# A token-mixing MLP on one core: tile 1 becomes a column group, w1 is loaded in a half and two quarters, and the order is planned anew

## The chip, the cores and the metric

The kernel runs on one core of a Trainium2 chip. The metric is the device time in microseconds (us). Times of the kernel before come from 13 runs and from one profiled execution.

## What is computed

x is [2048, 512] in bf16, w1 and w2 [512, 512], w3 [512, 1792], w4 [1792, 512].

```python
h = gelu(layernorm(x) @ w1)
c = D // 4                      # four column blocks, shifted along the tokens by 1, -1, 2, -2
g0 = pad(h[:, :, 0:c],     token shift +1)
g1 = pad(h[:, :, c:2*c],   token shift -1)
g2 = pad(h[:, :, 2*c:3*c], token shift +2)
g3 = pad(h[:, :, 3*c:],    token shift -2)
x1 = x + concatenate([g0, g1, g2, g3]) @ w2
out = x1 + gelu(layernorm(x1) @ w3) @ w4
```

The pads are written in short form; the layernorm has no weights and an eps of 1e-5.

## The kernel before

The 2048 tokens are 16 tiles of 128. A tile of layer 1 is numbered 0 to 15; the same tile of layer 2, after the mixing, 16 to 31. All inputs and intermediate results stay in SBUF.

Steps of a tile in layer 1: load x; mean and variance (`ln`, L379), on VectorE (`bnst`, `bnag`) or with two accumulating passes on ScalarE (`sum`, `ssq`, then `msq` and `vpe` on VectorE); `rstd` on GpSimd (L416); the normalised tile (`norm`), on VectorE, ScalarE or GpSimd, the latter two with `nmr` = -mean x rstd ahead; its transpose into `xnT`, by TensorE (`pe_transpose`, L459, evicted by `ev`) or by a DMA transpose from SP (L455); `mm_up` (L569), the product with w1 in groups of 1, 2 or 4 tiles, with a gelu into `hT` on ScalarE. `mm_mix` (L610) multiplies four shifted windows of `hT` with w2 and adds x on VectorE, then the same `ln` for layer 2, `mm_up` with w3 into `h2T`, and `mm_down` (L642) with w4, whose sum with x1 goes out by DMA.

Tiles listed in `NAT` take another way: they are only centred (`norm` without rstd), transposed, and multiplied the other way round (`mm_up_rows`, L513: four matmuls of 512 columns), so that rstd can be the scale of the gelu (`gelur`, L538); the result is then transposed on TensorE (`h_transpose`, L544, step `th`) and copied into `hT` (`evh`). Tile 0, in `SPLIT`, does its first steps in two halves (`sa`, `sb`, `ra`, `rb`).

The order comes from three hands:

- TensorE runs `SCRIPT` word for word: `warm:n` is n matmuls on zeros, `ty`/`sa`/`sb` are transposes on TensorE, `ra`/`rb` the rows of tile 0, `up1:g` and `up2:g` the groups of `GROUPS`, `mix:t`, `down:t`.
- `LOADS` gives the order of loads on SP (or ACT, with `@act`), with some DMA transposes as fixed points between them; a load that stands behind `tpN` isn't issued before that transpose is. Loads come first on SP otherwise (`op.first`, L703).
- VectorE, ScalarE, GpSimd and the other SP work are placed by `Program.order` and `Program.place`: every operation gets a latest start, counted back from the TensorE script with its durations and hops (`HOP`), and the engine takes the earliest latest-start among what is ready within `LOOK`. The planner's figures for loads are `BEGIN`, `LAG` and `RESTART`. What comes out is a fixed order on each engine; at run time semaphores alone decide when each starts.

Tables say which engine does what for each tile: `NORM` (VectorE where nothing is said), `EVAC` for the eviction of transposes (ScalarE where nothing is said), `STAT_ACT`, `NMR`, `HEV`.

Of the kernel before, what the change touches and what calls it, by code (L numbers as in the profile page):

```python
# [6 lines left out]
P = 128  # L7
# [18 lines left out]
class Program:  # L26
# [2 lines left out]

    HOP = {"pe": 200.0, "dve": 155.0, "act": 220.0, "pool": 120.0, "sp": 70.0}  # L30
    LOOK = {"dve": 300.0, "act": 300.0}
    DUE = 252723.0
    BEGIN = {"sp": 30.0, "act": 150.0, "pe": 400.0, "dve": 150.0, "pool": 450.0}
    ENTRY = 1900.0
    COLD, RESTART = 4300.0, 800.0
    LAG = {"load": 150, "tp": 700}

    def __init__(self):
        self.ops = []
# [111 lines left out]
    def place(self, succs, order_only):  # L151
# [46 lines left out]
        def land(op):  # L198
            nonlocal moved, last
            if op.queue == "tp":  # L200
                at = max(clock + 500.0, op.start + 2450.0, last + 600.0) + self.LAG["tp"]
            elif op.name.startswith("out"):
                at = clock + 300.0
                self.total = max(self.total, at)
            else:
                moved += op.dur
                at = clock + 600.0 + min(600.0, 0.3 * moved) + (600.0 if op.dur > 1400.0 else 0.0) + self.LAG["load"]
            if op.queue != "tp":
                last = max(last, at)
            op.landed = at  # L210
            for j in succs[op.idx]:
                if (op.idx, j) not in order_only:
                    release(op, self.ops[j], at + 30.0)

        while len(out) < len(self.ops):
            while True:
                best = None
                for e in ENGINES:
                    if cands[e]:
                        t = max(free[e], min(ready[o.idx] for o in cands[e]))  # L220
                        if best is None or t < best[0]:
# [12 lines left out]
            if op.queue:  # L234
                tp = op.queue == "tp"
                free[e] = start + (1300.0 if tp else 500.0)
                load = op.name.startswith("dma")
                work = 600.0 if tp else op.dur + (self.RESTART if load and not fed.get(e, True) else 0.0)
                fed[e] = load
                rings[e].append([start + (1400.0 if tp else 1000.0), work, op])  # L240
                for j in succs[op.idx]:
                    if (op.idx, j) in order_only:
                        release(op, self.ops[j], None)
            else:
                dur = op.dur
# [21 lines left out]
BIAS = {}  # L267
LOADS = """
x0 w1a w1b x4-5 w2b tp2 x3 w2a x6-7 w3b x8 w3a x1@act x9 x2@act x11 tp16 w4a x10 tp11 w4b tp9 x12-14 x15
"""  # L270
SCRIPT = """
warm:8 sa:0 sb:0 ty:1 ra:0 rb:0 up1:1 ty:2 th:0-1 up1:2 mix:0 ty:4 ty:3 mix:1 up1:3 ty:5 up1:4 mix:2 up1:5
mix:3 ty:17 mix:4 up2:0 up1:6 up2:1 mix:6 down:1 mix:5 up1:7-8 mix:8 mix:7 up1:9 mix:10 down:0 down:2 mix:9
up1:10 mix:12 mix:11 up2:2 mix:13 down:3 down:6 mix:14 up2:3 mix:15 down:4-5 down:7 down:11 down:9-10 up2:4
down:8 down:12 down:14 down:13 down:15
"""

def bass_standalone__mixer_s_mlp__prompt_kernel(nc, x, w1, w2, w3, w4, out):
# [14 lines left out]
    with ExitStack() as es:  # L293
# [37 lines left out]
        def pair_rv(p, v):  # L331
            return [(("y", p, 0), v), (("y", p, 1), v)]
# [26 lines left out]
        def load(item):  # L359
# [153 lines left out]
        def mm_up_rows(t):  # L513
# [3 lines left out]
            def part(c0, c1):  # L517
# [5 lines left out]

                return f

            if t in SPLIT:
# [11 lines left out]
            pg.add("act", f"gelur{t}",  # L538
                   lambda e: e.activation(hn[:, k, :], y_ps[:, p, 0:D], ACT_F.Gelu_apprx_tanh,  # L539
                                          scale=rstd[:, t : t + 1]),  # L540
                   reads=pair_rv(p, v) + [(("rstd", t), 0), (("warm",), 1)], writes=[(("hn", t), 0)], dur=50 + D * 0.833)
            yield

        def h_transpose(t, pair):  # L544
            g = group_of[1, t]
            how = HEV.get(t, "act")
            k = NAT.index(t)
            if pair:
                b, v = next_pair()
                res, dst = pair_rv(b, v), y_bf[:, b, 0:D]  # L550
            else:
                b, v = next_bank()
                res, dst = [(("o", b), v)], o_bf[:, b, 0:D]

            def f(e):
                for c in range(DC):
                    ins = e.transpose(dst[:, P * c : P * (c + 1)], hn[:, k, P * c : P * (c + 1)], ident[:])  # L557
                return ins

            pg.add("pe", f"th{t}", f, reads=[(("hn", t), 0), (("ident",), 1)], writes=res, dur=225)  # L560
            to, frm = hT[:, :, 2 + P * t : 2 + P * (t + 1)], dst.rearrange("p (c s) -> p c s", s=P)
            pg.add(how, f"evh{t}",
                   (lambda e: e.activation(to, frm, ACT_F.Copy)) if how == "act" else
                   (lambda e: e.tensor_copy(to, frm)),
                   reads=res, writes=[(("h", j, g), 0) for j in range(DC)],
                   dur=(60 + 0.82 * D) if how == "act" else (75 + 0.51 * D))


        def mm_up(layer, g):  # L569
            t0, n = groups[layer][g]  # L570
# [123 lines left out]
        steps = [s for s in steps if s[0] not in ("th", "tz") or s[1] in NAT]  # L694
# [13 lines left out]
        for kind, n in steps:  # L708
            if kind == "warm":
                warm_pe(n)  # L710
            elif kind in ("sa", "ra"):
                halves[kind[0], n] = pe_transpose(n, n, True) if kind == "sa" else mm_up_rows(n)
                next(halves[kind[0], n])
            elif kind in ("sb", "rb"):
                next(halves[kind[0], n])
            elif kind in ("tp", "ty"):
                run(pe_transpose(n % NT, n, kind == "ty"))
            elif kind in ("th", "tz"):
                h_transpose(n, kind == "tz")
            elif kind == "mix":  # L720
                mm_mix(n)
            elif kind == "down":
# [107 lines left out]
```

## Time and profile before

| | |
|---|---|
| median of 13 runs | 135.44 us (134.97 to 136.0) |
| the profiled execution | 135.58 us; its span 134.2 us |
| TensorE busy | 130.7 us (97%), 780 matmuls |
| VectorE, ScalarE, GpSimd busy | 51.9, 58.5, 25.8 us |
| HBM | 6.82 MB read, 2.10 MB written |

The span runs from the first instruction to the last; the time of the execution has 1.4 us around it. In views of the profile PE is a matmul, PEld a weight load, DVE VectorE, ACT ScalarE, POOL GpSimd, SP SyncE; a q behind a name is the engine's own queue of instructions that aren't counted as busy, such as DMA issues. A line of a timeline or chain gives the start and duration in us, the engine, the line of the kernel, the operation, its output and inputs; the bracket is the idle time before it and what ended it. The end of a matmul is modelled.

### The profile page before, as it was taken

To read this page: it belongs to the slowest core of one execution; us is meant where nothing else is said; L and a number is where in the kernel's file an instruction comes from. 1 tells how busy PE (TensorE), PEld (TensorE's weight loads), DVE (VectorE), ACT (ScalarE), POOL (GpSimd) and SP (SyncE) were. 2 spreads that over 40 slices of the span, in tenths; PEclk is the share of its full clock that TensorE was granted. 3 is DMA by queue.
4 is the path that set the end of the run, shared out by engine and by line. 5 is a ranking of instruction groups with operands and counts; after the bars stand their busy time and mean duration, and the time that the engine had idled before them with its cause. 6 is when DMAs were issued, how large, how long until landed. Compare 5 with 4: busy or idle time off the path is not lost.

```text
span 134.2 us, 2013 instructions
## 1 busy us (share of the span) xinstructions
PE 130.7 (97%) x780; PEld 72.8 (54%) x792; DVE 51.9 (39%) x140; ACT 58.5 (44%) x90; POOL 25.8 (19%) x59
## 2 busy tenths in 40 slices
PE   8989999999999999999999999999999999999994
PEld 3468688885576446444444444444444444444463
DVE  2889999304947737700053400062222200012222
ACT  5698985669394303785520366600000155520000
POOL 2534467600865301300010310010000000000000
PEclk9999999999999999999999999999999999999999
DMA  6999398599056542111003110003112100001112
GB/s 186 365 389 350 56 316 142 100 288 244 11 107 82 118 82 75 39 39 39 5 0 78 39 39 0 0 0 85 39 39 73 45 0 0 0 5 39 39 39 78
DMA packets 21897, 12.32 MB, mean 92 GB/s; under 512 B 14464, under 2 KB 21376, under 8 KB 21888
## 3 DMA queue, kind: packets, MB, share of 16 engines
q1 hardware_dynamic: 21168, 11.80, 33.1%
q10 hardware_dynamic: 720, 0.39, 1.0%
q8 instruction: 6, 0.10, 0.3%
q14 instruction: 3, 0.02, 0.1%
HBM read 6.82 MB, written 2.10 MB: 66 GB/s over the span
## 4 chain that ended last, share of the span: by engine, by line
PE 97%; issue 1%; ACT 1%; DVE 0%; POOLq 0%; ACTq 0%
PE y_ps L586 45%; PE o_ps L655 36%; PE o_ps L626 10%; PE o_ps L679 3%; PE y_ps L520 2%; PE y_ps L482 1%; ACT hn L539 1%; PE o_ps L557 0%; DVE o_sb L663 0%; POOLq L815 0%; ACTq L779 0%
## 5 line engine op out<-in xcount | busy, mean ns | idle before, releaser
L586 PE MATMUL y_ps<-xnT,w_sb 128*128 128x256 bf16 (+2 forms) x421 | 62.4, 306 | 0.2
L586 PEld LDWEIGHTS y_ps<-xnT,w_sb 128*128 128x128 bf16 x424 | 39.0, 98 | 23.4 <-DVE xnT L490 0.3
L655 PE MATMUL o_ps<-w_sb,h2T 128*128 128x512 bf16 (+2 forms) x247 | 49.0, 355 | 0.3
L601 ACT ACTIVATE h2T<-y_ps 128x1024 bf16<-128x1024 f32 (+1 forms) x29 | 28.6, 993 | 42.6 <-PE y_ps L586 42.6
L655 PEld LDWEIGHTS o_ps<-w_sb,h2T 128*128 128x128 bf16 x252 | 23.6, 98 | 25.2
L663 DVE TENSOR_TENSOR o_sb<-o_ps,x_sb 128x512 bf16<-128x512 f32 (+2 forms) x18 | 11.4, 632 | 40.0 <-PE o_ps L655 39.9
L416 POOL TENSOR_TENSOR rstd<-mv,neghalf 128x1 f32<-128x1 f32 x21 | 11.6, 554 | 42.5 <-DVE mv L411 38.5
L626 PE MATMUL o_ps<-w_sb,hT 128*128 128x512 bf16 x60 | 15.2, 379 | 0.3
L409 DVE BATCH_NORM_STATS2 st<-x_sb 128x6 f32<-128x512 bf16 x21 | 14.2, 675 | 2.3 <-DMA x_sb<-in_x_dram 2.2
L637 DVE TENSOR_TENSOR x_sb<-o_ps,x_sb 128x512 bf16<-128x512 f32 x10 | 6.9, 687 | 12.7 <-PE o_ps L626 12.7
L633 DVE SCALAR_TENSOR_TENSOR x_sb<-o_ps,x_sb 128x512 bf16<-128x512 f32 x6 | 4.1, 690 | 16.8 <-PE o_ps L626 16.8
L601 ACT ACTIVATE hT<-y_ps 128x1024 bf16<-128x1024 f32 (+1 forms) x9 | 7.4, 827 | 6.3 <-PE y_ps L586 6.2
L416 POOL TENSOR_TENSOR rstd<-vpe,neghalf 128x1 f32<-128x1 f32 x11 | 6.0, 550 | 18.8 <-DVE vpe L405 18.7
L626 PEld LDWEIGHTS o_ps<-w_sb,hT 128*128 128x128 bf16 x64 | 6.0, 98 | 5.5
L437 DVE TENSOR_SCALAR xn_buf<-x_sb,mv,rstd 128x512 bf16<-128x512 bf16 x15 | 7.0, 468 | 4.8 <-POOL rstd L416 4.6
L446 ACT ACTIVATE xn_buf<-x_sb,nmr,rstd 128x512 bf16<-128x512 bf16 x8 | 6.5, 811 | 5.1 <-DVE nmr L442 3.2
L393 ACT ACTIVATE junk<-x_sb 128x512 bf16<-128x512 bf16 x11 | 6.8, 622 | 2.7 <-DVE x_sb L633 2.7
L449 POOL TENSOR_SCALAR xn_buf<-x_sb,rstd,nmr 128x512 bf16<-128x512 bf16 x7 | 5.3, 763 | 0.8 <-DVE nmr L442 0.4
L679 PE MATMUL o_ps<-zeros 128*128 128x512 bf16 x8 | 3.6, 631 | 0.6 <-POOLq L815 0.6
L411 DVE BATCH_NORM_AGGREGATE mv<-st 128x2 f32<-128x9 f32 x21 | 4.0, 191 | 0.2
L388 ACT ACTIVATE junk<-x_sb 128x512 bf16<-128x512 bf16 x5 | 3.1, 624 | 0.3 <-DMA x_sb<-in_x_dram 0.3
L482 PEld LDWEIGHTS y_ps<-ident,xn_buf 128*128 128x128 bf16 x28 | 2.3, 111 | 1.3 <-issue 0.6
(35 smaller groups left out, 30.8 us busy)
## 6 DMA issues: line engine op xcount, KB each, us to landing
w_sb<-in_w_dram SPq DMA_DIRECT2D x4, 896.0 KB, 6.5
out_dram<-o_sb SPq DMA_DIRECT2D x15, 128.0 KB, 1.7
w_sb<-in_w_dram SPq DMA_DIRECT2D x4, 256.0 KB, 4.6
x_sb<-in_x_dram SPq DMA_DIRECT2D x7, 128.0 KB, 5.1
x_sb<-in_x_dram SPq DMA_DIRECT2D x2, 256.0 KB, 4.9
xnT<-xn_buf SPq DMA_TRANSPOSE x25, 2.5
x_sb<-in_x_dram SPq DMA_DIRECT2D x1, 384.0 KB, 4.8
x_sb<-in_x_dram ACTq DMA_DIRECT2D x2, 128.0 KB, 3.3
```

Source lines behind the costliest of these rows:

```text
L393: (lambda d: (lambda e: e.activation(d, src, ACT_F.Square, accum_out=sums[:, q, 1:2])))(junk[:, b, :]),
L409: pg.add("dve", f"bnst{q}", lambda e: e.bn_stats(st9[:, q, 0:6], src), reads=rs, writes=[(("st", q), 0)], dur=605)
L416: lambda e: e.tensor_tensor(col(rstd), var, neghalf[:], ALU.pow),
L437: lambda e: e.tensor_scalar(dst, src, mv[:, q, 0:1], rstd[:, q : q + 1], ALU.subtract, ALU.mult),
L446: f = lambda e: e.activation(dst, src, ACT_F.Identity, bias=nmr[:, q : q + 1], scale=rstd[:, q : q + 1])
L586: ins = e.matmul(y_ps[:, p, W * i : W * (i + 1)], wsb[:, dc, P * fc : P * (fc + 1)], src[:, dc, P * t0 : P * t0 + W], start=(dc == 0), sto ...
L601: (lambda d, s: (lambda e: e.activation(d, s, ACT_F.Gelu_apprx_tanh)))(dst, ysrc),
L626: ins = e.matmul(dst, hT[:, j, c0 : c0 + P], w2_sb[:, j, :], start=(j == 0), stop=(j == DC - 1))
L637: f = lambda e: e.tensor_tensor(x1_sb[:, t, :], dst, x_sb[:, t, :], ALU.add)
L655: ins = e.matmul(dst, h2T[:, fc, P * t : P * (t + 1)], w4_sb[:, fc, cs], start=(fc == 0), stop=(fc == FC - 1))
L663: (lambda d, c: (lambda e: e.tensor_tensor(o_sb[:, oi, c], d, x1_sb[:, t, c], ALU.add)))(dst, cs),
L679: ins = e.matmul(o_ps[:, b, :], zeros[:, 0:P], zeros[:], start=True, stop=True)
```

## The change

- `NAT` shrinks from tiles 0 and 1 to tile 0. Tile 1 is now normalised in full (on ScalarE), and goes through `mm_up` as a group of one tile, 16 matmuls of 128 columns; `th:1` is gone. The copy of tile 0 into `hT` moves from ScalarE to VectorE (`HEV`).
- The first loads on SP are x1 and x2; x0 comes over ACT's queue. w1 comes as its first half, its fourth quarter and its third quarter; w2 as a half and two quarters, w3 and w4 as quarters. x7 to x10 come as one load. No load ahead of w4 stands behind a DMA transpose any more (tile 16 is transposed on TensorE); only tp7 stands in the list, ahead of x13 to x15.
- The warming matmuls go from 8 to 11. ty:2 now stands before the rows of tile 0.
- Groups of layer 1: six single tiles, then 2, 4, 2, 2. Groups of layer 2: 2, 4, 4, 4, 2 instead of 2, 2, 4, 4, 4, so that down:0 follows up2:0 and mix:4.
- The engine tables and the planner's figures change, and with them the order that the planner finds. `CSPLIT` is empty, so the code for it does nothing; `h_transpose` is a generator now and always uses a bank of `o_ps`, as `th:0` did.

```diff
-    DUE = 252723.0
-    BEGIN = {"sp": 30.0, "act": 150.0, "pe": 400.0, "dve": 150.0, "pool": 450.0}
+    DUE = 198048.0
+    BEGIN = {"sp": 30.0, "act": 560.0, "pe": 400.0, "dve": 150.0, "pool": 450.0}
-    LAG = {"load": 150, "tp": 700}
+    LAG = {"load": 750, "tp": 700}
...
-                at = clock + 600.0 + min(600.0, 0.3 * moved) + (600.0 if op.dur > 1400.0 else 0.0) + self.LAG["load"]
+                at = clock + 600.0 + min(600.0, 0.3 * moved) + (600.0 if op.dur > 1400.0 else 0.0)
+                at += self.LAG["load"] if moved > 1200.0 else 50.0
...
-                work = 600.0 if tp else op.dur + (self.RESTART if load and not fed.get(e, True) else 0.0)
+                dry = load and not fed.get(e, True) and clock + sum(h[1] for h in rings[e]) < start + 800.0
+                work = 600.0 if tp else op.dur + (self.RESTART if dry else 0.0)
...
-GROUPS = {1: (1, 1, 1, 1, 1, 1, 2, 2, 2, 2, 2), 2: (2, 2, 4, 4, 4)}
-NORM = {4: "act", 5: "act", 6: "act", 10: "act", 11: "pool", 12: "pool", 13: "act", 15: "act", 18: "pool", 20: "pool", 21: "pool", 22: "pool", 24: "act", 28: "act", 30: "pool"}
-EVAC = {1: "both", 2: "dve", 3: "dve", 7: "both", 9: "dve", 10: "both", 11: "both", 13: "both", 16: "dve", 17: "both", 19: "both", 20: "dve", 22: "both", 23: "dve", 24: "dve", 25: "dve", 28: "dve", 31: "dve"}
-STAT_ACT = (1, 6, 8, 9, 12, 21, 22, 23, 27, 28, 29)
+GROUPS = {1: (1, 1, 1, 1, 1, 1, 2, 4, 2, 2), 2: (2, 4, 4, 4, 2)}
+NORM = {1: "act", 5: "act", 6: "pool", 7: "pool", 8: "act", 9: "act", 10: "act", 11: "pool", 13: "pool", 18: "pool", 20: "pool", 21: "pool", 24: "act", 27: "pool", 28: "pool", 29: "pool"}
+EVAC = {0: "dve", 1: "both", 4: "both", 5: "both", 6: "dve", 7: "dve", 8: "both", 9: "both", 10: "dve", 11: "both", 15: "both", 17: "dve", 19: "both", 20: "dve", 21: "dve", 24: "both", 25: "both", 29: "dve", 30: "both", 31: "dve"}
+STAT_ACT = (0, 6, 7, 8, 9, 12, 13, 18, 21, 22, 25, 27)
...
-NMR = {0: "pool", 1: "pool", 3: "pool", 5: "pool", 7: "pool", 9: "pool", 10: "pool", 12: "pool", 13: "pool", 14: "pool", 17: "pool", 18: "pool", 19: "pool", 21: "pool", 22: "pool", 23: "pool", 27: "pool", 30: "pool"}
-NAT = (0, 1)
+NMR = {0: "pool", 2: "pool", 3: "pool", 4: "pool", 5: "pool", 6: "pool", 7: "pool", 8: "pool", 14: "pool", 16: "pool", 18: "pool", 22: "pool", 25: "pool", 26: "pool", 28: "pool", 31: "pool"}
+NAT = (0,)
 SPLIT = (0,)
-HEV = {2: "dve", 5: "dve", 6: "dve"}
-BIAS = {}
+CSPLIT = ()
+HEV = {0: "dve", 1: "dve", 2: "dve", 4: "dve", 6: "dve"}
+BIAS = {"msq0": -366.448}
 LOADS = """
-x0 w1a w1b x4-5 w2b tp2 x3 w2a x6-7 w3b x8 w3a x1@act x9 x2@act x11 tp16 w4a x10 tp11 w4b tp9 x12-14 x15
+x1 x2 w1a w1s w1r x3 x4 w2b x0@act w2q w2p x5 x6 tp5 w3r w3s x7-10 tp4 w3p tp5 w3q w4q w4p tp16 x12 w4r x11
+w4s tp7 x13-14 x15
 """
 SCRIPT = """
-warm:8 sa:0 sb:0 ty:1 ra:0 rb:0 up1:1 ty:2 th:0-1 up1:2 mix:0 ty:4 ty:3 mix:1 up1:3 ty:5 up1:4 mix:2 up1:5
-mix:3 ty:17 mix:4 up2:0 up1:6 up2:1 mix:6 down:1 mix:5 up1:7-8 mix:8 mix:7 up1:9 mix:10 down:0 down:2 mix:9
-up1:10 mix:12 mix:11 up2:2 mix:13 down:3 down:6 mix:14 up2:3 mix:15 down:4-5 down:7 down:11 down:9-10 up2:4
-down:8 down:12 down:14 down:13 down:15
+warm:11 sa:0 sb:0 ty:1-2 ra:0 rb:0 up1:1 th:0 up1:2 mix:0 ty:3 mix:1 ty:4 up1:3-4 ty:5 mix:2 ty:16 mix:3
+ty:17 up1:5 up2:0 mix:4 down:0 up1:6 down:1 up1:7 mix:5-6 up1:9 mix:10 mix:9 up1:8 mix:8 mix:7 up2:1 mix:11
+mix:13 up2:2 mix:12 down:5 down:2-3 mix:15 up2:3 mix:14 down:6 down:13 down:9 up2:4 down:4 down:10 down:7
+down:11 down:8 down:12 down:14-15
 """
...
-                c0, c1 = {"": (0, n), "a": (0, n // 2), "b": (n // 2, n)}[name[2:]]
+                cut = lambda k: k * n // 4
+                a, b = {"": (0, 4), "a": (0, 2), "b": (2, 4), "p": (0, 1), "q": (1, 2), "r": (2, 3), "s": (3, 4)}[name[2:]]
+                c0, c1 = cut(a), cut(b)
...
-        def h_transpose(t, pair):
+        def h_transpose(t):
```

A `tpN` in `LOADS` whose tile is transposed by TensorE is passed over (L698 to L700).

More of the change, by code (lines that the diff above doesn't have):

```diff
@@ L524, in part, with f @@
                 return f
+            if t in CSPLIT:
+                H = D // 2
+                for hh in (0, 1):
+                    cs = slice(H * hh, H * (hh + 1))
+                    def f(e, hh=hh, cs=cs):
+                        for dc in range(DC):
+                            ins = e.matmul(y_ps[:, p, 512 * hh : 512 * hh + H], xnT[:, dc, P * t : P * (t + 1)],
+                                           w1_sb[:, dc, cs], start=(dc == 0), stop=(dc == DC - 1))
+                        return ins
+                    pg.add("pe", f"rows{t}_{hh}", f,
+                           reads=[(("w1", c), 0) for c in range(DC)] + [(("xT", t, c), 1) for c in range(DC)],
+                           writes=[pair_rv(p, v)[hh]], dur=DC * 109.2)
+                    pg.add("act", f"gelur{t}_{hh}",
+                           (lambda a, b: (lambda e: e.activation(a, b, ACT_F.Gelu_apprx_tanh,
+                                                                 scale=rstd[:, t : t + 1])))(
+                               hn[:, k, cs], y_ps[:, p, 512 * hh : 512 * hh + H]),
+                           reads=[pair_rv(p, v)[hh], (("rstd", t), 0), (("warm",), 1)], writes=[(("hn", t, hh), 0)],
+                           dur=50 + H * 0.833)
+                    yield
+                return
             if t in SPLIT:
@@ L540, in mm_up_rows @@
                                           scale=rstd[:, t : t + 1]),
-                   reads=pair_rv(p, v) + [(("rstd", t), 0), (("warm",), 1)], writes=[(("hn", t), 0)], dur=50 + D * 0.833)
+                   reads=pair_rv(p, v) + [(("rstd", t), 0), (("warm",), 1)],
+                   writes=[(("hn", t, hh), 0) for hh in (0, 1)], dur=50 + D * 0.833)
             yield
-        def h_transpose(t, pair):
+        def h_transpose(t):
             g = group_of[1, t]
@@ L547, in h_transpose @@
             k = NAT.index(t)
-            if pair:
+            if t in CSPLIT:
                 b, v = next_pair()
-                res, dst = pair_rv(b, v), y_bf[:, b, 0:D]
+                steps = [(2 * hh, 2 * hh + 2, [pair_rv(b, v)[hh]], f"_{hh}") for hh in (0, 1)]
+                dst = y_bf[:, b, :].rearrange("p (k x) -> p k x", k=2)[:, :, 0 : D // 2]
+                chunk = lambda c: dst[:, c // 2, P * (c % 2) : P * (c % 2 + 1)]
+                part = lambda c0, c1: dst[:, c0 // 2, :].rearrange("p (c s) -> p c s", s=P)
@@ L551, in h_transpose @@
             else:
                 b, v = next_bank()
[L553 to L566, printed above, removed]
+                steps = [(0, DC, [(("o", b), v)], "")]
+                dst = o_bf[:, b, 0:D]
+                chunk = lambda c: dst[:, P * c : P * (c + 1)]
+                part = lambda c0, c1: dst.rearrange("p (c s) -> p c s", s=P)
@@ new lines, in h_transpose, with f @@
+            for c0, c1, res, tag in steps:
+                def f(e, c0=c0, c1=c1):
+                    for c in range(c0, c1):
+                        ins = e.transpose(chunk(c), hn[:, k, P * c : P * (c + 1)], ident[:])
+                    return ins
+                n = c1 - c0
+                pg.add("pe", f"th{t}{tag}", f,
+                       reads=[(("hn", t, hh), 0) for hh in range(c0 // 2, c1 // 2)] + [(("ident",), 1)],
+                       writes=res, dur=56 * n if n < DC else 225)
+                to, frm = hT[:, c0:c1, 2 + P * t : 2 + P * (t + 1)], part(c0, c1)
+                pg.add(how, f"evh{t}{tag}",
+                       (lambda a, b: (lambda e: e.activation(a, b, ACT_F.Copy)) if how == "act" else
+                        (lambda e: e.tensor_copy(a, b)))(to, frm),
+                       reads=res, writes=[(("h", j, g), 0) for j in range(c0, c1)],
+                       dur=(60 + 0.82 * n * P) if how == "act" else (75 + 0.51 * n * P))
+                yield
@@ L693, in bass_standalone__mixer_s_mlp__prompt_kernel @@
             steps += [(kind, n) for n in (range(int(a), int(b or a) + 1) if kind != "warm" else [int(n)])]
[L694 removed]
+        steps = [s for s in steps if s[0] != "th" or s[1] in NAT]
         pe_tp = {n for kind, n in steps if kind in ("tp", "ty", "sa")}
@@ L710, in bass_standalone__mixer_s_mlp__prompt_kernel @@
                 warm_pe(n)
-            elif kind in ("sa", "ra"):
-                halves[kind[0], n] = pe_transpose(n, n, True) if kind == "sa" else mm_up_rows(n)
+            elif kind in ("sa", "ra", "ta"):
+                halves[kind[0], n] = {"s": lambda n: pe_transpose(n, n, True), "r": mm_up_rows,
+                                      "t": h_transpose}[kind[0]](n)
                 next(halves[kind[0], n])
-            elif kind in ("sb", "rb"):
+            elif kind in ("sb", "rb", "tb"):
                 next(halves[kind[0], n])
@@ L717, in bass_standalone__mixer_s_mlp__prompt_kernel @@
                 run(pe_transpose(n % NT, n, kind == "ty"))
-            elif kind in ("th", "tz"):
-                h_transpose(n, kind == "tz")
+            elif kind == "th":
+                run(h_transpose(n))
             elif kind == "mix":
```

## The prediction

> **What bounds the kernel now.** I read the page's chain first (who ends last), then the chain in order of time (where it breaks), then the timeline of the first 9 us (why).
>
> ```profile
> PE 97%; issue 1%; ACT 1%; DVE 0%; POOLq 0%; ACTq 0%
> ```
>
> The end is set by TensorE alone; no other engine owns over 1% of the 134.2 us span. The chain in order of time shows where it isn't dense:
>
> ```profile
> 0.64 3.60 PE o_ps L679 x8
> 4.24 0.85 PE y_ps L482 x8
> 5.09 2.12 PE y_ps L520 x8
> ...
> 7.29 0.70 ACT hn L539
> ...
> 8.03 0.40 PE o_ps L557 x4
> 8.43 0.89 PE y_ps L586 x16
> 9.32 0.10 issue
> 9.42 0.81 PE o_ps L626 x3
> ...
> 17.26 13.97 PE y_ps L586 x128
> ```
>
> Prices per matmul follow: 128 columns 0.89/16 = 0.0556 us; 256 columns 13.97/128 = 0.109; 512 columns 0.2157 (14 of L655 in 3.02). From 9.32 (mix:0; an "issue" ahead of an "x3" is a matmul missing from the records) to 17.26 (up2:0) are 5 mixes (4.31), 4 tile transposes (0.90) and 3 single-tile ups (2.68): 7.89 of 7.94 us. From 17.26 to 132.41 the work priced so is 115.1 of 115.15 us. So **only the stretch before 9.32 holds idle PE time**: warming to 4.03, the wait of th1 for its gelu (7.2 to 8.03), and slow matmuls: 8 transposes take 0.85 instead of 0.45 us, 8 row matmuls 2.12 instead of 1.73.
>
> ```profile
> 2.61 0.69 DVE L409 BATCH_NORM_STATS2 st<-x_sb 128x6 f32<-128x512 bf16 x1 [2.02 <-DMA x_sb<-in_x_dram]
> 2.91 0.63 ACT L388 ACTIVATE junk<-x_sb 128x512 bf16<-128x512 bf16 x1 [0.31 <-DMA x_sb<-in_x_dram]
> 3.33 0.20 DVE L411 BATCH_NORM_AGGREGATE mv<-st 128x2 f32<-128x9 f32 x1
> 3.69 0.66 POOL L416 TENSOR_TENSOR rstd<-mv,neghalf 128x1 f32<-128x1 f32 x1 [1.99 <-DVE mv L411]
> 4.47 0.69 DVE L409 BATCH_NORM_STATS2 st<-x_sb 128x6 f32<-128x512 bf16 x1 [0.16 <-DMA x_sb<-in_x_dram]
> 5.44 0.11 PEld L520 LDWEIGHTS y_ps<-w_sb,xnT 128*128 128x128 bf16 x1 [0.31 <-DMA w_sb<-in_w_dram]
> 8.71 0.21 DVE L442 TENSOR_SCALAR nmr<-mv,rstd 128x1 f32<-128x1 f32 x1 [0.17 <-POOL rstd L416]
> 8.96 0.81 ACT L446 ACTIVATE xn_buf<-x_sb,nmr,rstd 128x512 bf16<-128x512 bf16 x1
> ```
>
> The last two lines are of a later tile, for the time that nmr and a ScalarE norm take. SP's first load (x0) is used at 2.61, ACT's first (x1) at 2.91, ACT's second (x2) at 4.47, w1's second half at 5.44.
>
> **What the Trainium skill says.** "TensorE: Matmul & The Clock Gate", Part 1: the array starts at half clock and is released by a free-running window of about 3.4 us, so the moment varies from run to run; cold 106.7/426.7 ns, warm 55.6/215.7 ns at 128/512 columns. The trace agrees: warming matmuls start 0.42 to 0.43 us apart, the transposes at 4.03 are 0.107 apart, and full pace comes only near 5.6. "Perfetto Trace Analysis", Tensor Engine Instruction: VectorE, ScalarE and GpSimd are strict FIFO; on this rests all I say of a wait holding what is queued behind it. "DMA: Bandwidth & Descriptors", Queues, rings and completion order: the DMA engines take turns between the SP and ACT rows. That fits x0 landing at 2.6 and x1 at 2.9.
>
> **The change, part by part.**
>
> *Start.* I follow the planner's rule (lowest latest-start first) by hand for the order on the engines, and take times from the trace only. x1 is now SP's first load: landed for use at 2.61. x0 is ACT's first: 2.91. x2 is SP's second: bounded by x1's 2.91 from below and by 4.47, what x2 took as ACT's second, from above. I take 3.6: the 393 KB of x0, x1, x2 are through about 2.7 by the page's GB/s, and landings trail by 0.7 to 1.2 us. VectorE: stats of x1 2.61 to 3.53, stats of x2 (0.69) to 4.29, then nmr1, which waits for rstd1 (3.69 + 0.66 = 4.35, + 0.10): 4.45 to 4.66; the mean of x2 to 4.75; norm0 in two halves to 5.15; norm2; ev0's halves. Queued behind the waiting nmr1 are that mean, norm0 and norm2, so sa:0, ty:2 and ra:0 wait for it.
> - ty:1: norm1 is now full and on ScalarE: 4.71 + 0.81 = 5.52, PE at 5.65. Before, centred-only on VectorE, done at 4.31.
> - ty:2: rstd2 4.9 to 5.45, norm2 (0.41) to 5.95, PE 6.1 to 6.3.
> - ra:0: ev0's first half runs after norm2, to 6.2; so rows at 6.3, before 5.02. Loss 1.3 us.
>
> *Warm 8 to 11.* Three more at 0.427 cold: 1.28 us, from 4.03 to 5.33 (0.65 if the clock has come). Norm0 allows sa:0 only at about 5.05, and ty:1 at 5.65; four half-transposes of 0.107 fit between, so the price is nothing. Cover gone: up to 1.28 us.
>
> *Tile 1 as a column group.* Four row matmuls (4 x 0.2157 = 0.86), gelur1 (0.69) and th1 (4 x 0.0556 = 0.22) go; 16 matmuls of 128 columns (0.89) come. Rows 6.3 to 7.16; up1:1 to 8.05 covers gelur0 (7.25 to 7.95, as gelur1 now follows its matmuls by 0.08); th0 to 8.27; up1:2 to 9.16. evh0, now on VectorE (0.42 instead of 0.60), is done by 8.9. So mix:0 starts at 9.16 to 9.3, before 9.32: **the removed gelu wait and cold pace (0.8 + 0.8) pay for the later start (1.3) and little more.** Gain 0.1.
>
> *tp16 to PE.* One tile transpose more after mix:0: + 0.22. Its DMA (SP issue 1.27) no longer stands ahead of w4.
>
> *Groups.* Two 256-column groups become one of 512 in layer 1: 32 x 0.1092 - 16 x 0.2157 = 0.04 gained. Up2 has the same 112 and 168 matmuls, reordered; downs, mixes and tail are the same count.
>
> *Loads.* w1 has the same seven 128 KB units ahead of its end, so it lands at about 5.43 as before; ra:0 and rb:0 need it at 6.3 and 6.7, so the split is worth 0 (cover gone: the excess over 6.7). One 128 KB unit costs (14.25 - 2.59)/32 = 0.364 us (33 units by x11's landing). w2 ends with unit 13, 7.0 to 7.9, needed at 9.2. w3 ends with unit 33, 14.3, needed at 16.4. w4 is no longer held behind tp16 and tp11; it ends with unit 49: 2.59 + 48 x 0.364 = 20.1. down:0 now comes right after up2:0 and mix:4 (16.4 + 6.1 + 0.9 = 23.4): cover 3.3 us. Moved past SP's queue: transposes follow all those loads; tp6 and tp7 are needed at 26.4, tp8 to tp11 at 31.2, at 1.3 us each. x13 to x15 wait behind tp7, needed only by up1:9 near 36. Cost 0 to 0.5; I take 0.
>
> *VectorE, 6.7 to 15.3.* ty:17 is due there at 15.3. Spaced as in the trace (stats 0.75, norm 0.33, x1 0.60, half eviction 0.20), stats of 3, 4, 5, 16, 17 (3.75), norms of 3, 4, 16, 17 (1.32), evh0 (0.34), three x1 (1.8) and two evictions (0.4) make 7.6 of 8.6 us; with waits for rstd I get ty:17 at 15.45. Cost 0 to 0.5, I take 0.15. Other stat, norm and rstd moves on ScalarE and POOL lie under 6 us of up2:0.
>
> *Sum* against the profiled execution (span 134.2, time 135.58): - 0.10 + 0.22 - 0.04 + 0.15 = **+0.2**, so 135.8. But that execution lies 0.14 over the median of 13 (135.44), and its slow clock lasted to 5.6 us, which costs the old order about half of the overlap with its work and the new one, which idles then, nothing. The early terms are good to 0.2 only; I write 135.5.
>
> **The rivals.** About 0.27 us (0.2%) is what a measurement of this kernel can tell from no change.
> - *Forecast: a tie*, 135.2 to 135.7. Chance 0.42.
> - *The start is quicker than my order.* If the mean of x2 goes ahead of nmr1, rstd2 starts at 4.35, norm2 ends at 5.45, rows start at 6.0 (ty:1 then limits) and no VectorE delay follows: 0.3 + 0.15 less, with tile 16's transpose in a gap of PE another 0.2: 135.5 - 0.5 = 135.0. For: POOL is free there. Against: nmr1 has the earlier due time. Chance 0.30.
> - *x2 lands late.* In VectorE's FIFO the stats of x2 stand before nmr1. From a landing of 3.76 on (4.45 - 0.69) each later us is lost once: at 4.47, as now, nmr1 is at 5.2, rows at about 7.0: + 0.7, 136.2; half as late 135.9. For: x2 took 3.8 us from issue in this trace. Against: it was second on ACT, now second on SP. With VectorE's delay at ty:17 it is the slower side. Chance 0.28.
> - *The w1 split is what it says but does nothing*: inside the tie.
>
> **How the numbers follow.** Chances are those of the three cases: faster 0.30, same 0.42, slower 0.28. The range reaches to 134.9 (quick start) and 136.2 (x2 as late as now); a w4 or transpose stall beyond is left out.
>
> **What would show it.** Rows (L520, four) starting near 6.3; mix:0 (first L626) near 9.2; up2:0 about 16.5; no DMA wait at the first L655 (down:0) near 23.4. Wrong if rows start below 5.9 or above 6.8, if PE waits for VectorE before ty:17 over 0.4 us, or if any wait breaks the chain after 17 us.

## The result, and where the time went

| | before | after |
|---|---|---|
| median | 135.41 us (134.95 to 136.14, 48 runs) | 137.02 us (136.22 to 138.37, 11 runs) |
| ratio | | 1.0119, 95% interval 1.0098 to 1.0141 |
| span, median of the runs | 134.1 to 134.4 us (by set of runs) | 135.4 us (134.5 to 136.5) |
| time around the span | 1.3 to 1.4 us | 1.3 us in 4 of 12 runs, 1.7 to 1.9 in 8 |
| profiled execution | 135.58 us, span 134.2 | 136.22 us, span 134.5 |

The change made the kernel slower by 1.6 us: 1.0 to 1.3 of span (by the set of runs of before that is taken), and 0.3 on average around it. Ratios and spans leave out the few executions in a slower state (here one of 12), while medians of the time keep them. The profiled execution of after happens to be the fastest of its runs, so it shows the loss in small; a repeat of the same kernel, below, shows it at its usual size.

The page's chain of after, shares of the span by engine:

```profile
PE 90%; ACT 4%; DVE 2%; DMA 2%; issue 1%; POOL 0%; DVEq 0%; SPq 0%
```

Before, TensorE had 97% here. The chain now leaves it in the first 17 us. The same chain in order of time, early and then around 16 us (start, duration, what):

```profile
0.09 2.36 DMA x_sb<-in_x_dram
4.41 0.82 ACT xn_buf L452
5.92 0.95 PE y_ps L526 x4
6.87 0.89 PE y_ps L624 x16
9.05 0.81 PE o_ps L664 x3
```

```profile
15.03 0.61 ACT junk L399 x2
15.63 0.62 ACT junk L394 x2
16.26 0.22 issue
16.48 6.27 PE y_ps L624 x56
```

The rows of tile 0 (L526, L520 before) start at 5.81 by the timeline, the first recorded matmul of mix:0 (L664) at 9.05, where before had it at 9.42, and up2:0 (the x56) at 16.48: close to the prediction's 6.3, 9.2 and 16.5. That up2:0 meets its forecast is luck, since a start 0.3 to 0.4 us quicker than forecast and a wait that wasn't forecast cancel. It could have started at 16.09, when the last matmul of up1:5 was issued and had run; TensorE stood for 0.39 us. The chain names ScalarE's statistics pass (L394) as what came before it. That pass is not an input of up2:0. The DMA view of the loads that SP issued between 7.82 and 7.90 us (only w3's last quarter; KB, then us from issue to landing) gives the real releaser:

```profile
w_sb<-in_w_dram SPq DMA_DIRECT2D x1, 448.0 KB, 8.3
```

Issued at 7.83, it landed at 16.13, where the prediction had w3 at 14.3. TensorE went on about 0.3 us later.

### The profile page after: what moved, and what is told of

Same layout as the page of the kernel before. It is cut to its first block, busy times and chain, and to the rows that moved or that the text cites. A ratio compares the mean times of both kernels' runs of the same rounds, so it can differ in the third digit from the quotient of the medians.

```text
span 134.5 us, 2020 instructions
## 1 busy us (share of the span) xinstructions
PE 131.0 (97%) x779; PEld 71.6 (53%) x791; DVE 52.0 (39%) x143; ACT 57.6 (43%) x92; POOL 27.6 (21%) x60
## 4 chain that ended last, share of the span: by engine, by line
PE 90%; ACT 4%; DVE 2%; DMA 2%; issue 1%; POOL 0%; DVEq 0%; SPq 0%
PE y_ps L624 43%; PE o_ps L693 36%; PE o_ps L664 9%; DMA x_sb<-in_x_dram 2%; ACT junk L399 1%; ACT junk L394 1%; PE y_ps L488 1%; PE y_ps L526 1%; ACT xn_buf L452 1%; ACT xnT L496 1%; DVE x_sb L671 1%; DVE st L415 1%; ACT hT L639 0%; POOL rstd L422 0%; DVE mv L417 0%
## 5 line engine op out<-in xcount | busy, mean ns | idle before, releaser
L624 PE MATMUL y_ps<-xnT,w_sb 128*128 128x512 bf16 (+2 forms) x420 | 63.6, 308 | 0.4 <-ACT junk L394 0.2
L624 PEld LDWEIGHTS y_ps<-xnT,w_sb 128*128 128x128 bf16 x424 | 38.3, 98 | 25.0 <-DVE vpe L411 0.4
L693 PE MATMUL o_ps<-w_sb,h2T 128*128 128x512 bf16 (+2 forms) x248 | 48.9, 355 | 0.2
L693 PEld LDWEIGHTS o_ps<-w_sb,h2T 128*128 128x128 bf16 x252 | 23.5, 98 | 24.9 <-issue 0.4
L675 DVE TENSOR_TENSOR x_sb<-o_ps,x_sb 128x512 bf16<-128x512 f32 x11 | 7.5, 684 | 22.0 <-PE o_ps L664 22.0
L664 PE MATMUL o_ps<-w_sb,hT 128*128 128x512 bf16 x60 | 14.9, 379 | 0.2
L415 DVE BATCH_NORM_STATS2 st<-x_sb 128x6 f32<-128x512 bf16 x20 | 13.6, 685 | 2.7 <-DMA x_sb<-in_x_dram 2.5
L639 ACT ACTIVATE hT<-y_ps 128x512 bf16<-128x512 f32 (+1 forms) x10 | 8.1, 810 | 6.6 <-PE y_ps L624 6.5
L664 PEld LDWEIGHTS o_ps<-w_sb,hT 128*128 128x128 bf16 x64 | 6.1, 98 | 6.0
L399 ACT ACTIVATE junk<-x_sb 128x512 bf16<-128x512 bf16 x12 | 7.5, 623 | 2.7 <-DVE x_sb L671 2.6
L455 POOL TENSOR_SCALAR xn_buf<-x_sb,rstd,nmr 128x512 bf16<-128x512 bf16 x10 | 7.6, 766 | 1.0 <-DVE nmr L448 0.4
L452 ACT ACTIVATE xn_buf<-x_sb,nmr,rstd 128x512 bf16<-128x512 bf16 x6 | 4.8, 811 | 0.9 <-DVE mv L417 0.9
L717 PE MATMUL o_ps<-zeros 128*128 128x512 bf16 x11 | 4.2, 558 | 0.6 <-POOLq L854 0.6
L394 ACT ACTIVATE junk<-x_sb 128x512 bf16<-128x512 bf16 x7 | 4.4, 623 | 0.7 <-DMA x_sb<-in_x_dram 0.7
L488 PE MATMUL y_ps<-ident,xn_buf 128*128 128x128 bf16 x32 | 3.0, 220 | 0.2 <-ACT xn_buf L452 0.2
```

Source lines behind the costliest of these rows:

```text
L399: (lambda d: (lambda e: e.activation(d, src, ACT_F.Square, accum_out=sums[:, q, 1:2])))(junk[:, b, :]),
L415: pg.add("dve", f"bnst{q}", lambda e: e.bn_stats(st9[:, q, 0:6], src), reads=rs, writes=[(("st", q), 0)], dur=605)
L452: f = lambda e: e.activation(dst, src, ACT_F.Identity, bias=nmr[:, q : q + 1], scale=rstd[:, q : q + 1])
L455: f = lambda e: e.tensor_scalar(dst, src, rstd[:, q : q + 1], nmr[:, q : q + 1], ALU.mult, ALU.add)
L624: ins = e.matmul(y_ps[:, p, W * i : W * (i + 1)], wsb[:, dc, P * fc : P * (fc + 1)], src[:, dc, P * t0 : P * t0 + W], start=(dc == 0), sto ...
L639: (lambda d, s: (lambda e: e.activation(d, s, ACT_F.Gelu_apprx_tanh)))(dst, ysrc),
```

## Where the loads fell behind

SP's timeline, before and then after: SP issues a load every 0.47 us or so, for 128 KB as for 896 KB.

```profile
0.09 0.40 SPq L365 DMA_DIRECT2D x_sb<-in_x_dram  x1
0.56 0.93 SPq L372 DMA_DIRECT2D w_sb<-in_w_dram  x2
1.53 0.47 SPq L365 DMA_DIRECT2D x_sb<-in_x_dram  x1
...
4.05 0.47 SPq L372 DMA_DIRECT2D w_sb<-in_w_dram  x1
```

```profile
0.09 0.87 SPq L369 DMA_DIRECT2D x_sb<-in_x_dram  x2
1.00 1.45 SPq L378 DMA_DIRECT2D w_sb<-in_w_dram  x3
2.49 0.91 SPq L369 DMA_DIRECT2D x_sb<-in_x_dram  x2
3.44 1.42 SPq L378 DMA_DIRECT2D w_sb<-in_w_dram  x3
4.89 0.91 SPq L369 DMA_DIRECT2D x_sb<-in_x_dram  x2
5.85 0.91 SPq L378 DMA_DIRECT2D w_sb<-in_w_dram  x2
```

The first part of w3 is issued at 4.05 us before and at 5.85 after. By 2.45 us the two queues of before had been given 1408 KB (x0 to x2, w1, x4-5, w2b), those of after 768 KB (x0 to x2, w1). The windows view shows what the DMA engines made of it; of each line read the last two figures, the DMA share and GB/s, before and then after:

```profile
2.00:3.00 1.00, 1.00 (x4) 0.35 (x3) 0.39 (x1) 0.68 (x3) 0.00 (x0) 1.00 1.06 346
3.00:4.00 1.00, 1.00 (x3) 0.18 (x2) 0.93 (x5) 1.00 (x3) 0.31 (x1) 1.00 1.03 356
4.00:5.00 1.00, 1.00 (x9) 0.84 (x9) 0.84 (x3) 0.76 (x4) 0.35 (x1) 1.00 1.07 375
```

```profile
2.00:3.00 1.00, 1.00 (x4) 0.34 (x3) 0.53 (x1) 0.33 (x2) 0.00 (x0) 1.00 0.81 241
3.00:4.00 1.00, 1.00 (x3) 0.30 (x2) 0.93 (x3) 0.52 (x2) 0.52 (x1) 1.00 0.68 174
4.00:5.00 1.00, 1.00 (x8) 0.46 (x6) 0.67 (x4) 0.59 (x1) 0.57 (x2) 1.00 1.00 325
```

In these three microseconds 1077 KB came before and 740 KB after: 0.34 MB, at before's 350 GB/s about 1 us of loading, is missing from then on. "DMA: Bandwidth & Descriptors", Issuing engines are not separate DMA queues, of the Trainium skill says that the time a sequencer needs to initiate a DMA is "usually small relative to the DMA itself". For 128 KB this case says otherwise: 0.47 us of issue against 0.36 us of data. That the issues are what kept the engines short here is not shown by this: a kernel with fewer of them, below, loads no faster in this stretch.

## The experiments

The theories, by the letters that some of the expectations use. D: the many small early loads make w3 and w4 late, and TensorE waits for them. N: over 64 loads and stores lengthen the time around the span. V and E: VectorE or ScalarE is late for up2:0, as the profile's lines say. C: the cold clock at the start. Each ratio is to the kernel before, with its 95% interval; the span is the median of the runs. The experiments add lines, so L624, L664 and L693 are L625, L666 and L695 in some.

**The kernel after again.** No edit.

> The changed kernel once more, unaltered, for a second profile, since the first profiled execution (span 134.5 us) was the shortest of twelve, whose spans reach 136.7. Median about 137.0 again. Theory W (the last quarter of w4 lands too late for down:0): a longer execution shows PE waiting for a DMA of w4 ahead of the first matmul of L693, 0.5 to 2 us. Theory C (the array's clock is released later than before, because the new start leaves TensorE idle or only transposing between 4.8 and 5.8): the first L717, L488 and L526 matmuls are at half pace until 7 us or later, and nothing waits at L693. Theory E (ScalarE and VectorE late ahead of up2:0): PE waits near 13 to 16.5 us for ScalarE, by more than the 0.4 us of the first profile.

137.19 us, 1.0115 (1.0073 to 1.0157), span 135.4, which is 1.0 over the kernel before in the same set of runs. The timeline of this run again blames another engine:

```profile
17.11 0.56 PEld L624 LDWEIGHTS y_ps<-xnT,w_sb 128*128 128x128 bf16 x6 [0.67 <-DVE x_sb L675]
17.14 0.71 PE L624 MATMUL y_ps<-xnT,w_sb 128*128 128x256 bf16 x5 [0.52 <-DVE x_sb L675]
```

The sum of L675 belongs to another tile than the two of up2:0. w3's last quarter, issued at 7.80, landed 9.0 us later, at 16.8; TensorE had been free since 16.45 (0.68 us, the bracket leaves out a matmul missing from the records).

**Waits taken away by other data.** The first kernel lets down:0 use w4's chunks 3 to 6 in place of 10 to 13; the second lets up2:0 use w3's chunk 0 in place of chunk 1; the third does both. The work of every engine and its order stay the same; what is left out is the wait for the loads of the chunks replaced. Of the edits only the operands are shown; the lists of what these matmuls wait for are shortened to match.

```diff
-    w4_sb[:, fc, cs]
+    w4_sb[:, fc - 7 if t == 0 and fc > 9 else fc, cs]
```
```diff
+    wc = 0 if layer == 2 and g == 0 and dc == 1 else dc
-    wsb[:, dc, P * fc : P * (fc + 1)]
+    wsb[:, wc, P * fc : P * (fc + 1)]
```

> The changed kernel, but down:0 multiplies its last four chunks with four other chunks of w4 (3 to 6), so that it doesn't wait for w4's last quarter; every load and the order of all engines stay. Tile 0's output is another one for this. Theory W: the excess goes, 135.4 to 135.8 us. Theories C and E: 137.0 us, within 0.3 of the changed kernel.

> The changed kernel, but up2:0 multiplies with chunk 0 of w3 in place of chunk 1, so that it doesn't wait for the quarter that lands last; every load and the order of all engines stay. Tiles 0 and 1 of the output are others for this. Theory D: PE's gap ahead of up2:0 shrinks to under 0.1 us, the median falls by 0.3 to 0.7, to about 136.5 us, if w4 doesn't take the time back at down:0. Theory V: no change, 137.0 us.

> The changed kernel with both waits for weights taken away: up2:0 as in the run with chunk 0 for chunk 1 of w3, and down:0 with chunks 3 to 6 of w4 for 10 to 13. Tiles 0 and 1 of the output are others for this. Theory D with w4 as a second late landing: median 135.6 to 136.1 us, the span's median within 0.3 us of the kernel before; what then is left over is the time around the span (1.3 or 1.8 us in the runs of the changed kernel, 1.3 in all of before). Theory V: 136.7 us, as with down:0 alone.

| free of | median | ratio | span | over before in the same set |
|---|---|---|---|---|
| w4's last quarter at down:0 | 136.72 us | 1.0069 (1.0044 to 1.0095) | 135.0 | 0.6 |
| w3's last quarter at up2:0 | 136.6 us | 1.0066 (1.003 to 1.0101) | 134.85 | 0.75 |
| both | 136.07 us | 1.0032 (1.0008 to 1.0055) | 134.45 | 0.35 |

With w4's wait alone gone, up2:0 still stood for 0.43 us in the profiled execution; w3 landed at 16.05 there.

TensorE's timeline with w3's wait gone: at 15.89 up1:5 now runs straight into up2:0, but down:0 (L695) starts 0.50 us after the end of mix:4 (the first of mix:4's four matmuls is missing; the bracket again names a bystander). w4's last quarter landed at 24.1 there.

```profile
15.89 1.93 PE L625 MATMUL y_ps<-xnT,w_sb 128*128 128x128 bf16 x24
...
23.11 0.81 PE L666 MATMUL o_ps<-w_sb,hT 128*128 128x512 bf16 x3
24.25 1.02 PE L695 MATMUL o_ps<-w_sb,h2T 128*128 128x512 bf16 x4 [0.33 <-DVE xn_buf L443]
```

With both gone it is dense:

```profile
15.31 7.17 PE L625 MATMUL y_ps<-xnT,w_sb 128*128 128x128 bf16 x72
22.53 0.81 PE L666 MATMUL o_ps<-w_sb,hT 128*128 128x512 bf16 x3
23.25 2.10 PE L695 MATMUL o_ps<-w_sb,h2T 128*128 128x512 bf16 x9
```

V and E fall: VectorE and ScalarE do the same work in the same order in all four kernels, and the stall at up2:0 goes with w3's semaphore alone. C falls as the cause of the loss: by the spacing of the matmuls full pace came near 5.6 us in the profiled execution of before and near 5.8 in the repeat of after, and the kernel with four pairs joined, next, starts as this repeat does (first recorded matmul of mix:0 at 9.40 and 9.42) without the loss. The moment does move from run to run: where w3's wait is gone full pace came only near 6.5, and mix:0 at 9.75. The two waits are worth 0.65 us of span together by the sets' own runs of before (1.0 to 0.35), 0.95 by the medians as they stand (135.4 to 134.45).

**Early pairs joined.** w1's two quarters, x3 and x4, w2's two quarters, x5 and x6 become one load each (64 loads and stores instead of 68). Every engine keeps its order.

`join` (its code is left out) gives the first load of a pair the range of both and drops the second, after the order has been planned.

```diff
+        for a, b in [('w1s', 'w1r'), ('x3', 'x4'), ('w2q', 'w2p'), ('x5', 'x6')]:
+            join(a, b)
```

> The changed kernel with the order of every engine kept, but four pairs of neighbouring loads on SP joined into one DMA each: w1's third and fourth quarter, x3 and x4, w2's two quarters, x5 and x6. Theory D (SP issues one load per 0.48 us whatever its size, so that ten loads of 128 KB ahead of w3 keep the DMA engines short of work, w3's last quarter lands at 16.1 to 16.8 us, and up2:0 waits for it): w3 is issued some 1.9 us earlier and lands 0.8 to 1.2 us earlier, PE's gap ahead of up2:0 (0.4 to 0.7 us) goes, and the median falls by 0.5 to 1.0, to 136.0 to 136.5 us. Theory V (VectorE and ScalarE are late ahead of up2:0, as the chain names them): the gap and 137.0 us stay.

135.81 us, 1.0027 (1.0011 to 1.0044), span 134.5, 0.4 over before in the same set: in the profiled execution TensorE doesn't wait ahead of up2:0 or down:0. The loads of w3 and w4 joined into halves instead, with the early ones left small, do much less:

> The changed kernel with the four pairs of quarters of w3 and w4 joined, and the small loads ahead of w3 left as they are (64 DMAs; w4's last quarter goes ahead of x11 by this). The order of all engines stays. Theory D: w3 is issued as late as in the changed kernel, so it lands no earlier than 16 us and PE waits ahead of up2:0 as there, span 135.0 to 135.4; with theory N 1.3 us around it, 136.4 us in all. Rival (the number of loads alone counts): as with the four early pairs joined, 135.8 us.

136.46 us, 1.0091 (1.0054 to 1.0128), span 135.15, 0.95 over before. w3 landed at 16.70 in the profiled execution, as theory D says, and up2:0 waited 0.26 us.

**Which pair?** Only w1's quarters joined, and only the other three pairs.

> The kernel after with only the two quarters of w1 joined (67 loads and stores instead of 68), every engine's order as it is. If the loss is in proportion to the issues that SP spends on small loads ahead of w3, one of the four that the joined kernel saved is saved here: span about 135.1 to 135.2 instead of 135.4, time about 136.7 to 136.9. If the split of w1 is itself the cause (its last quarter starves the rows and what follows), the span falls to the 134.5 of the kernel with four joins, and the time to about 135.9. If w1 is nothing to it, 137.1 as the kernel after.

> The kernel after with x3 and x4, the two quarters of w2, and x5 and x6 joined, w1 left in its half and two quarters (65 loads and stores). In proportion to the issues: span about 134.7, time 136.0 to 136.2. If w1's split is the cause: span 135.4, time 136.8 or more. The two runs together say whether the split that the change is named for is the costly one.

135.92 us, 1.0034 (1.0015 to 1.0053), span 134.55, and 135.95 us, 1.0043 (1.0025 to 1.0062), span 134.6. Taken alone, the first is what "w1's split is the cause" had foretold, and the second comes close to a sum over issues; together neither holds. It is no sum, since one join gives as much as three or four, and w1's split is not *the* cause, since the kernel that keeps it is as fast. It looks like a threshold. (The traced execution of the kernel with only w1 joined is one of its longest, 135.1 us of 133.9 to 135.2: up2:0 still waits 0.61 us there.)

**What the joins change.** D, as I had it, is at most half of the story. The trace keeps, for each load, when each of its 16 parts was complete. The table has, for the profiled execution of each kernel, the GB/s of 0 to 6 us and of 8 to 12 us (windows view), and for the last load of w3 its place among the loads of SP, when most of it was there (the 14th of the 16 parts) and when all of it was (us):

```
kernel                      0-6  8-12  place  most   last   last - most
before                      267  401   11th   12.95  13.69  0.74
before, early splits        232  336   15th   14.63  15.61  0.98
after                       209  346   17th   15.62  16.13  0.51
after again                 192  359   17th   15.40  16.79  1.38
free of w4 at down:0        202  353   17th   15.19  16.05  0.87
free of w3 at up2:0         212  300   17th   16.21  17.11  0.90
free of both                214  313   17th   15.86  18.07  2.21
w3 and w4 joined            196  314   15th   16.41  16.70  0.29
only w1 joined              196  375   16th   14.93  16.68  1.75
w2, x3-4, x5-6 joined       213  366   14th   15.53  15.81  0.28
four pairs joined           207  390   13th   15.19  15.40  0.21
four pairs, 9 warming       201  392   13th   14.95  15.01  0.05
four pairs, 8 warming       211  398   13th   14.97  15.26  0.30
```

The first 6 us are not what the joins mend. The kernels with the new order load 192 to 214 GB/s there with the pairs joined and without, against 267 before; over 6 us that is 0.3 to 0.45 MB, or about 1 us of loading at 350 GB/s. The windows of the kernel with four pairs joined, to be set beside those of after above:

```profile
2.00:3.00 1.00, 1.00 (x4) 0.33 (x3) 0.42 (x1) 0.24 (x2) 0.00 (x0) 1.00 0.76 231
3.00:4.00 1.00, 1.00 (x3) 0.30 (x2) 0.97 (x3) 0.61 (x2) 0.42 (x1) 1.00 0.78 201
4.00:5.00 1.00, 1.00 (x4) 0.43 (x3) 0.74 (x5) 0.49 (x1) 0.57 (x2) 1.00 1.02 331
```

By 2.45 us this kernel had been given 1152 KB, where after had 768, and it moved no more. So the early shortage is not shown to come from small loads. A rival is the order of the first loads: x2 now stands behind x1 on SP instead of on ACT's queue, and w1 behind both. No run changed that alone, so the cause of the early shortage stays open.

What goes with the joins comes later. From 8 to 12 us four joined pairs load at 390 to 398 GB/s and fewer joins at 366 and 375, against 300 to 359 without early joins. And the last parts come sooner. One or two of the sixteen parts lag behind the others by up to 2.2 us. The lag is not one load's: it rises at one, and then stays at about the same size for those that follow (1.61 to 1.78 us over ten loads where only w1 is joined) until it is gone at w4's last quarter. Without early joins (but for w3 and w4 joined), and with only w1 joined, it rises between SP's 12th and 14th load, ahead of w3's end; with three or four pairs joined it rises at the 15th (w4: 0.22 to 0.93 us with four pairs), behind w3's end. TensorE was ready for w3 at 16.0 to 16.7 us where it had to wait, so most of the parts came in time or nearly so, and in most of these kernels the lag decides. The early shortage explains why the cover is thin, the late parts why it is then exceeded. The kernel before has late parts too, 0.7 us in its profiled execution; w3 lands there at 13.7, over 3 us ahead of its use.

The same loads can give different lags: 0.51, 1.38 and 0.87 us in the three kernels that load exactly as after does up to w3's end and wait for it, and 0.7 us in before but 0.2 in the kernel below that differs from it only in late loads. So chance has a share, and with one traced execution for each kernel the place where the lag rises is an observation, not a law. Why it rises when it does wasn't isolated. "DMA: Bandwidth & Descriptors", Latency and other measured facts, of the Trainium skill says that two of the sixteen DMA engines, 7 and 15, are usually slower than the others; its guess at the cause is limited to DMAs issued by GpSimd, which these loads are not. One or two late parts fit that, but the records don't say which engine did which part.

**The same splits in the kernel before.** w1b, x4-5, w2a and x6-7 become two loads each (67 loads and stores instead of 63), orders kept.

> The kernel before with four of its early loads cut in two: w1's and w2's second in line into quarters, x4-5 and x6-7 into single tiles (67 DMAs), the order of all engines kept. Theory D (small loads keep the DMA engines short of work): the DMA engines have moved some 0.15 to 0.3 MB less by 7 us, w3's last half lands 0.5 to 1 us later than 13.7, but up2:0 needs it only at 17.1, so the span stays within 0.3 us. With theory N 1.8 us around the span in half of the runs. Rival (w3's late landing comes from the order of the loads, not from their size): landing at 13.7 as before.

136.95 us, 1.0084 (1.0053 to 1.0116), span 135.3 against 134.2. w3 landed at 15.6, 1.9 us later for 0.5 to 1 expected, and still in time; the loss came by another load, which I hadn't thought of. ScalarE's timeline, before and then with the splits:

```profile
14.69 0.62 ACT L388 ACTIVATE junk<-x_sb 128x512 bf16<-128x512 bf16 x1
15.21 0.19 ACT L388 ACTIVATION_READ_ACCUMULATOR junk<-x_sb 128x1 f32 x1
15.35 0.60 ACT L601 ACTIVATE hT<-y_ps 128x512 bf16<-128x512 f32 x1
```

```profile
16.03 0.63 ACT L388 ACTIVATE junk<-x_sb 128x512 bf16<-128x512 bf16 x1 [1.22 <-DMA x_sb<-in_x_dram]
16.56 0.19 ACT L388 ACTIVATION_READ_ACCUMULATOR junk<-x_sb 128x1 f32 x1
16.66 0.58 ACT L601 ACTIVATE hT<-y_ps 128x512 bf16<-128x512 f32 x1
```

ScalarE waits for x9, which landed at 14.0 before and at 16.0 now; behind it in the queue stands the gelu that mix:4 needs, and TensorE stands 1.19 us before mix:4. Here most of x9's parts are late (15.0 instead of 13.3), and the lag adds 1.0 instead of 0.7. Nothing differs but the splits, and both stretches of the table are slower: splitting early loads is costly in this order too, by whatever use comes due first.

**Number of loads and stores.** In the kernel before, x12-14 as three loads and the outputs of three tiles in halves: 68 in all, those added late.

> The kernel before with five more DMAs where nobody is in a hurry: x12 to x14 as three loads, and the outputs of tiles 0, 2 and 3 in two halves each; 68 DMAs, as many as the changed kernel has, against 63. The order of all engines stays. Theory N (over 64 DMAs in a program add 0.45 us around the span to about half of the executions: the changed kernel's runs show 1.3 or 1.8 us there, those of before and of the kernel with joined loads, 64 DMAs, 1.3 alone): span as before (134.1 to 134.4), 1.8 us around it in half of the runs, median up by 0.1 to 0.4. Rival: the time around the span has to do with the early loads, then 1.3 in all runs and a ratio of 1.000.

135.73 us, 1.0013 (0.9996 to 1.003), the span unchanged (134.25), the time around it 1.28 to 1.60 us, median 1.5, against 1.3 to 1.4. Over all kernels: 1.25 to 1.41 us in every run with 63 to 65; with 67 or 68 often 1.5 to 1.9, also with the early splits above (1.57 to 1.69). But the kernel with only w1 joined has 67, and 1.3 to 1.4 us in all its runs. N is thus no rule: the count alone does not set it. What does stays open; it is worth 0.3 us of the 1.6. w1 split alone in the kernel before, which might tell, wasn't tried.

**Fewer warming matmuls**, with the four pairs joined: 9, then 8 instead of 11.

> The changed kernel with the four early pairs of loads joined and 9 warming matmuls for 11. In the trace of the kernel with joined loads TensorE is dense from 0.63 us to the end, but it spends up to 5.3 us on warming while norm0 is ready at 4.6. The order of all engines stays. Theory: the rows start 0.2 us earlier, span 134.3 for 134.5, median 135.6; not below the kernel before, since the transpose of tile 16 on TensorE (0.22 us) stays. Rival: warming shorter, the clock's release comes later and the gain goes, 135.8 or more.

> Four joins and 8 warming matmuls, as in the kernel before, instead of 11. Going from 11 to 9 gave 0.17 us. If each warming matmul in the way of the first transposes costs its share, 8 give 0.05 to 0.2 more: 135.45 to 135.6, level with the kernel before or a little under it. If the first transposes wait for the norms of tile 0 by then, nothing more: 135.64.

135.64 us, 1.0005 (0.9991 to 1.0018), and 135.6 us, 1.0011 (0.9996 to 1.0027); both spans are 0.1 over before, where 11 had 0.4. TensorE's timeline with four pairs joined, with 11 and then with 8:

```profile
5.29 1.01 PE L488 MATMUL y_ps<-ident,xn_buf 128*128 128x128 bf16 x12
6.19 1.02 PE L526 MATMUL y_ps<-w_sb,xnT 128*128 128x512 bf16 x4
```

```profile
4.74 1.32 PE L488 MATMUL y_ps<-ident,xn_buf 128*128 128x128 bf16 x12 [0.50 <-DVE xn_buf L433]
5.95 1.02 PE L526 MATMUL y_ps<-w_sb,xnT 128*128 128x512 bf16 x4
```

The rows come 0.24 us earlier; 9 already give it, and then the norms of tile 0 set the start. With this the new order is level with the old one. No version beat the kernel before.

## Why the prediction was wrong, step by step

- **Loads: "Cost 0 to 0.5; I take 0." This is the step that failed.** It has w3's end at 14.3 and 2.1 us of cover ahead of up2:0. w3 landed at 16.1 in the profiled execution and at 16.8 in the repeat, TensorE stood for 0.39 and 0.68 us, and a late w4 came on top; without the two waits the span is 0.65 to 0.95 us shorter. Two things were wrong in the sum. The unit price, 0.364 us for 128 KB, came from the stream of before, with 267 GB/s over the first 6 us; the new list has 192 to 214 there, and so a landing about 1 us later, with small loads or joined ones. And a landing is that of the last of 16 parts: behind the 14th the last came 0.5 to 2.2 us later where no early pairs and no quarters of w3 were joined, and the price held 0.7 of that. Together they used up the cover. "The split is worth 0" was right for the rows that use w1, which ran without a gap. It was wrong for what stands behind it in the queue: joining the quarters of w1 alone, or the other three pairs, gives back 0.5 us of span or more. How much of the early shortage is due to the order and how much to the sizes stays open. The lag can be read in the trace of before: 0.7 us between the 15th and 16th part of most of its early loads.
- **w4, "cover 3.3 us".** Its last quarter landed at 22.8 instead of 20.1, against down:0 at 23.6. It cost nothing in the profiled execution of after, but 0.4 us of span in the median by the run that is free of it, and 0.5 us where up2:0 didn't wait first.
- **"No DMA wait at the first L655"** was the sign that I named. I named none for up2:0, where I had the smaller cover: the wait that decides came 7 us ahead of the one that I watched.
- **Start, rows, tile 1 as a column group:** right in the main, with a spread that I hadn't given. x2 landed at 3.1, so that the rival of a late x2 fell; nmr of tile 1 went ahead of x2's mean, as worked out by hand. Rows started at 5.81, below the 5.9 that I had named as a sign of being wrong, and at 6.21 in the repeat; over the traced kernels with this start and 11 warming matmuls at 5.7 to 6.5. Like for like, the first recorded matmul of mix:0 came at 9.05 and 9.42, for 9.42 before. One reading was off without consequence: the gelu wait of th:1 was 0.56 us, not 0.8, since th:0 ran from 7.25 to 7.47 in that stretch.
- **Warm 8 to 11, "the price is nothing":** wrong by 0.2 to 0.3 us. By the prediction's own figures warming ends at 5.33, and four transposes of 0.107 behind it end at 5.76, past the 5.65 that they were to fit ahead of.
- **VectorE, 0.15:** nothing of it came. In the profiled executions of after and of its repeat TensorE has no gap ahead of ty:17.
- **The sum of TensorE's terms, + 0.2:** right in size. With the load waits gone, by other data or by joins, the span is 134.45 to 134.6, 0.35 to 0.5 over the kernel before in the same sets of runs; with 8 or 9 warming matmuls it is 0.1 over. That the warming left out and the 0.15 that didn't come nearly cancel is luck.
- **Rivals.** A quick start did come (rows at 5.81 in the profiled execution) and was lost in the wait at up2:0. The slower side, which I gave 0.28, came by a mechanism that I had priced at 0, and went past the range's 136.2: the range had a load stall "left out" in so many words. The around-the-span time, 0.3 us, was in no step at all.

## What to carry to other kernels

When loads are split or moved, work out anew when every load behind them lands; a price taken from the old stream need not hold for the new one. The bill comes at the use that has the thinnest cover, not at the load that was split. Take for the landing the last of its sixteen parts, and leave it a cover as large as the lag that the trace shows, or more. When several semaphores stand ahead of a matmul, believe the profile's releaser only if the named result is an input of it; else take the wait away with other data and see. And look for an explanation's mark in the stretch where it is said to act: the joins gave the time back, but not the early loading rate that I had explained by the small loads.

## What the runs showed of the hardware that was not expected

- SP issued a load about every 0.47 us in the first 7 us, for 128 KB as for 896 KB, so 128 KB loads from SP alone come at 270 GB/s at most (128 KB in 0.48 us), where the larger ones of before reached 346 to 390. Fewer and larger loads did not raise the rate of the first 6 us in the new order.
- One or two of a load's 16 parts can be late by 0.2 to 2.2 us, at a constant size over ten loads, and by different amounts in executions with the same loads.
- The time around the span is not a constant of the chip: 1.3 us in most kernels here, up to 1.9 in some; more loads and stores often, but not always, go with it.
- Behind the landing that ended its wait, up2:0 started 0.25 to 0.36 us later in five traced executions; ScalarE's pass over x9 started 0.03 us behind its landing, and down:0 0.13 us.
